# Second expert product of batches 1 to 3 as seven block products with block sums, experts summed in PSUM, gates in the relu outputs

## Chip, cores, metric

The kernel runs on one core of one Trainium2 chip. Times are device microseconds (us) of whole executions, given as the median over the runs of a kernel; executions of one kernel mostly agree within 0.5%. The profile's span, from the first to the last instruction, is about 2 us shorter than the time.

Names: PE is TensorE (PEld its weight loads), DVE is VectorE, ACT is ScalarE, POOL is GpSimd, SP is SyncE. The granted clock is the share of its full speed that PE was allowed. The chain of waits is the work that ended last, followed back at each step to what released it. In all the listings "L592" is a line of the kernel in question, so line numbers differ between kernels.

## The reference, cut to what matters

Sliding-window attention with four sink positions over 4 batches of 768 tokens gives x of 3072 x 512. Then a mixture of four experts, all of them used by every token:

```python
p = domain_probs / (domain_probs.sum(-1, keepdims=True) + 1e-09)   # [3072, 4], never negative
for e in range(4):
    h = np.maximum(x @ w1[e], 0.0)          # 512 -> 1024
    out += p[:, e:e + 1] * (h @ w2[e])      # 1024 -> 512
```

## The kernel before

The kernel interleaves two strands on PE: the attention of the next batch and the two expert products of this batch. A small planner in the Python code keeps a believed clock for each engine and decides, while the program is built, in which order the instructions are recorded. Each engine then executes its own list strictly in that order.

The first product makes h transposed (1024 features on partitions, tokens in the free dimension), the relu writes it to SBUF as `ht`, and the second product uses `ht` as weights, so tokens come out on the partitions, where the gate is one number for a partition:

```python
def emit_first(self):                     # 384 tokens in batches 1 to 3, 256 in batch 0
    for db in range(NDB):
        nc.tensor.matmul(hp_, lhsT=w1_sb[e][:, db, fb*P:(fb+1)*P], rhs=xT[b, db][:, t0:t0+n], ...)
    # relu on whichever of ACT and DVE is believed free first
    ...
def emit_second(self):
    for fb in range(NFB):
        nc.tensor.matmul(op, lhsT=hts[fb][:, off:off+P], rhs=w2_sb[e][:, fb, :], ...)   # 512 columns
    # gate and sum over experts, on DVE, from PSUM:
    nc.vector.scalar_tensor_tensor(out=dst, in0=op, scalar=sc, in1=dst, op0=ALU.mult, op1=ALU.add)
    ...
```

The attention's path from PE to PE crosses DVE twice: the exponentials are multiplied by a mask (`aT`), and the values are divided by their sum (`onat`). PE needs both before it can go on with that strand.

The softmax here doesn't subtract the row's maximum and nothing guards it: scores larger than these inputs give would overflow.

Of the kernel before, what the change touches and what calls it, by code (L numbers as in the profile page):

```python
# [16 lines left out]
def kernel(  # L17
# [42 lines left out]
    PARTS = {b: [(0, G), (G, G), (2 * G, G)] if b == 0 else [(0, 3 * P), (3 * P, 3 * P)] for b in range(B)}  # L60

# [6 lines left out]
    t = {"pe": 0.0, "act": 0.0, "dve": 0.0}  # L68
    bank_free = {tag: [0.0] * n for tag, n in (("mix", 1), ("od", 2), ("h", 2), ("o", 2))}
# [9 lines left out]
    def dve(cols, *deps, rate=0.96):  # L79
        t["dve"] = max(t["dve"], *deps) + 130 + cols / rate  # L80
        return t["dve"] + 60

# [21 lines left out]

    ctx.enter_context(tc.manual_schedule())
# [5 lines left out]
    def load_qk(b, piece):  # L111
        s0, T = PIECES[b][piece]
        for name, src in (("q", q), ("k", k)):
            x = sb.tile([P, H, T * D], BF16, name=f"{name}n", tag=f"{name}n", bufs=1)
            nc.gpsimd.dma_start(
                out=x, in_=src[b, :, s0:s0 + P * T, :].rearrange("h (p t) d -> p h (t d)", t=T),
            )
            nat[b, piece, name] = x
        lands(("qk", b, piece), 2 * H * P * T * D * 4)

    def load_first():

        s0, T = PIECES[0][0]
        for half in range(2):
            hs = slice(4 * half, 4 * half + 4)
            for name, src in (("q", q), ("k", k)):
                x = mo.tile([P, 4, T * D], FP32, name=f"{name}raw", tag=f"osb{half}", bufs=2)
                nc.sync.dma_start(
                    out=x, in_=src[0, hs, s0:s0 + P * T, :].rearrange("h (p t) d -> p h (t d)", t=T),
                )  # L130
                nat[0, half, name, "raw"] = x
            lands(("first", half), 2 * 4 * P * T * D * 4)
# [14 lines left out]
    def regroup(b, piece):  # L147

        s0, T = PIECES[b][piece]
        for name in "qk":  # L150
            x = sb.tile([P, T, H, D], BF16, name=f"{name}o", tag=f"{name}o", bufs=1)
            engine, at = sooner(T * H * D, landed["qk", b, piece], rate=1.9)
            copy(engine, x, nat[b, piece, name].rearrange("p h (t d) -> p t h d", t=T))
            nat[b, piece, name] = x
            grouped[b, piece] = max(at, grouped.get((b, piece), 0))

    def regroup_first():
        s0, T = PIECES[0][0]
        for name in "qk":
            nat[0, 0, name] = sb.tile([P, T, H, D], BF16, name=f"{name}f", tag=f"{name}f", bufs=1)  # L160
        for half in range(2):
            at = max(act(512, landed["first", half]), dve(512, landed["first", half]))
            for name in "qk":
                copy(
                    "act" if name == "k" else "dve",
                    nat[0, 0, name][:, :, 4 * half:4 * half + 4, :],
                    nat[0, half, name, "raw"].rearrange("p h (t d) -> p t h d", t=T),
                )
        grouped[0, 0] = at

    vx = []
    for i in range(2):
        vx.append(consts.tile([P, NQB, H, DP], BF16, name=f"vx{i}"))

    def load_v(b, ts):
        for tb in ts:
            nc.gpsimd.dma_start(  # L177
                out=vx[b % 2][:, tb, :, 0:D],
                in_=v[b, :, tb * P:(tb + 1) * P, :].rearrange("h p d -> p h d"),
            )  # L180
            lands(("v", b, tb), H * P * D * 4)
# [12 lines left out]

    load_first()
    NT = Ntok // P
    dp = consts.tile([NT, P, E], FP32, name="dp")
    nc.sync.dma_start(out=dp, in_=moe_domain_probs.rearrange("(tb p) e -> tb p e", p=P))


    zeros = consts.tile([P, 2 * G], BF16, name="zeros")
# [12 lines left out]
    for i in range(2):  # L214
        nc.vector.memset(vx[i][:, :, :, D:DX], 1.0)
# [44 lines left out]
    vsd = consts.tile([P, B, NHP, 2, DX], BF16, name="vsd")  # L260
# [20 lines left out]
    qkT, xT, sinkA, aTs, onats = {}, {}, {}, {}, {}  # L281
    turned_at, sinkA_at, aT_at, onat_at, xT_at = {}, {}, {}, {}, {}

    def two_banks(tag="mix"):
# [4 lines left out]
        return [psum.tile([P, 2 * G], FP32, name="sps", tag=tag) for _ in range(2)], None  # L289

    def transposes(b, piece, hp, tag="mix"):

        s0, T = PIECES[b][piece]
        if (b, hp) not in qkT:
            qkT[b, hp] = sb.tile([P, 2, S], BF16, name="qkT", tag="qkT", bufs=5)
        tr = psum.tile([P, 2, T, P], BF16, name="tr", tag=tag, bufs=1 if tag == "mix" else 2)
        for i, name in enumerate("qk"):
            for tt in range(T):
                nc.tensor.transpose(tr[:, i, tt], nat[b, piece, name][:, tt, 2 * hp:2 * hp + 2, :], ident)  # L299
        done = pe(2 * T * P, grouped[b, piece], free_at(tag))  # L300
# [8 lines left out]
    def sink_keys(b):  # L309
        for hp in range(NHP):  # L310
            nc.gpsimd.tensor_mul(  # L311
# [3 lines left out]
            )  # L315

    def sink_values(b):
        nc.gpsimd.tensor_mul(
            vsd[:, b], vsf[:, b, None, None, :].to_broadcast([P, NHP, 2, DX]), sel2,
        )  # L320

    def sinks(b, piece):

        if b not in sinkA:
            sinkA[b] = sb.tile([P, 2 * G], BF16, name="sinkA", tag="sinkA", bufs=2)
# [11 lines left out]
        done = pe(q1 - q0 + 300, free_at("mix"), *[turned_at[b, piece, hp] for hp in range(NHP)])  # L337
# [42 lines left out]
    def values(b, hp, g, tag="od"):  # L380

        ready = values_ready(b, hp, g, tag)
        od = psum.tile([P, 2, 2, DX], FP32, name="od", tag=tag)
        a = aTs.pop((b, hp, g))
        cols = 0
        for qi in range(2):
# [7 lines left out]
            if g > 0:  # L394
                nc.tensor.matmul(  # L395
                    od[:, qi], lhsT=sinkA[b][:, (qb - 2) * P:(qb - 1) * P], rhs=vsd[:, b, hp],
# [3 lines left out]
            for ph in range(2):  # L400
                for i, (kb, c) in enumerate(terms):
                    nc.tensor.matmul(  # L402
                        od[:, qi, ph], lhsT=a[:, ph, c:c + P], rhs=vx[b % 2][:, kb, 2 * hp + ph, 0:DX],
# [11 lines left out]
        onats[b, hp, g], onat_at[b, hp, g] = o, at  # L415

    def values_ready(b, hp, g, tag="od"):
        return max(
            aT_at[b, hp, g], free_at(tag), sinkA_at.get((b, g), 0.0), landed["v", b, 2 * g + 1],
        )  # L420

    def turn(b, hp, g, tag="od"):

        o = onats.pop((b, hp, g))
        tx = psum.tile([P, 2, P], BF16, name="tx", tag=tag)
# [10 lines left out]
    def turn_ready(b, hp, g, tag="od"):  # L436
        return max(onat_at[b, hp, g], free_at(tag))

    class Attention:
# [11 lines left out]
        def options(self):  # L451
# [5 lines left out]
            if self.todo:  # L457
# [4 lines left out]
                elif kind == "regroup":  # L462
                    yield max(landed["qk", b, x], t["pe"]), "todo"
                elif kind == "transposes":
                    yield max(grouped[b, x], free_at("mix")), "todo"
                elif kind == "sinks":
                    yield max([free_at("mix")] + [turned_at[b, x, hp] for hp in range(NHP)]), "todo"

        def emit(self, step):
# [7 lines left out]
            else:  # L477
# [4 lines left out]
                elif kind == "regroup":  # L482
                    regroup(b, x)
                    if b > 0:
                        sink_values(b)
                elif kind == "transposes":
                    transposes(b, x, y)
                elif kind == "sinks":
                    if b > 0:
                        sink_keys(b)  # L490
                    sinks(b, x)

# [3 lines left out]
    def gates():  # L496
        pt = psum.tile([P, E, NT], FP32, name="pt", tag="o")
# [9 lines left out]
        take("o", dve(600, pe(400, free_at("o"))))  # L507

    HT = 20
    out_sb = {}  # L510

    class Mixture:


        def __init__(self):
            self.first = [
                (b, e, part, fb) for b in range(B) for e in range(E)
                for part in range(len(PARTS[b])) for fb in range(NFB)
            ]
            self.second, self.hts, self.live, self.since = [], [], 0, 0  # L520
            self.done = 0.0

        def more(self):
            return bool(self.first or self.second)

        def first_ready(self):
            if not self.first or self.live >= HT:
                return 1e12
            b, e, part, fb = self.first[0]
            t0, n = PARTS[b][part]  # L530
            xs = [xT_at.get((b, hp, g), 1e12) for hp in range(NHP) for g in range(t0 // G, (t0 + n - 1) // G + 1)]
            return max(free_at("h"), landed["w1", e], *xs)

        def second_ready(self):
            if not self.second:
                return 1e12
            b, e, tb, hts, off, at = self.second[0]
            return max(free_at("o"), landed["w2", e], at)

        def emit_first(self):  # L540
            b, e, part, fb = self.first[0]
            t0, n = PARTS[b][part]
            ready = self.first_ready()
            self.first.pop(0)
            hp_ = psum.tile([P, n], FP32, name="hps", tag="h")
            for db in range(NDB):
                nc.tensor.matmul(  # L547
                    hp_, lhsT=w1_sb[e][:, db, fb * P:(fb + 1) * P],
                    rhs=xT[b, db][:, t0:t0 + n],
                    start=(db == 0), stop=(db == NDB - 1),  # L550
                )
            end = pe(NDB * n, ready)
            ht = mo.tile([P, n], BF16, name="ht", tag="hT", bufs=HT)
            engine, at = sooner(n, end)
            if engine == "act":
                nc.scalar.activation(out=ht, in_=hp_, func=AF.Relu)  # L556
            else:
                nc.vector.tensor_scalar(out=ht, in0=hp_, scalar1=0.0, scalar2=None, op0=ALU.max)  # L558
            take("h", at)
            self.hts.append((ht, at))  # L560
            self.live += 1
            self.since += 1
            self.done += NDB * n
            if fb == NFB - 1:
                hts = [x[0] for x in self.hts]
                at = max(x[1] for x in self.hts)
                self.hts = []
                for s in range(n // P):
                    self.second.append((b, e, t0 // P + s, hts, s * P, at))

        def emit_second(self):
            ready = self.second_ready()
            b, e, tb, hts, off, _ = self.second.pop(0)
            if (b, 0) not in out_sb:
                for i in range(2):
# [130 lines left out]
```

## Time and profile before

| | before |
|---|---|
| time, median of 3 runs | 420.5 us |
| span of the profiled run | 417.9 us |
| PE / DVE / ACT / POOL busy | 398.6 / 176.0 / 188.7 / 50.1 us |
| mean granted clock of PE | 0.980 |

The page of the kernel before: the span, the first part (busy us of each engine, its share, and the number of instructions) and the engines of the chain of waits.

```profile
span 417.9 us, 7002 instructions
PE 398.6 (95%) x2874; PEld 229.3 (55%) x2918; DVE 176.0 (42%) x349; ACT 188.7 (45%) x336; POOL 50.1 (12%) x94
PE 91%; DMA 3%; ACT 2%; POOL 1%; DVE 1%; issue 1%; ACTq 0%
```

PE is busy 95% of the time and is 91% of the chain, so the kernel is bound by PE and everything else has room. The timeline of PE in a late stretch, where no attention is left (columns: start, duration, engine, line, operation, output and inputs, count):

```profile
331.11 1.89 PE L582 MATMUL mop<-w,ht 128*128 128x512 bf16 x8
332.83 2.91 PE L547 MATMUL hps<-xT,w 128*128 128x384 bf16 x16
335.58 1.89 PE L582 MATMUL mop<-w,ht 128*128 128x512 bf16 x8
```

From the starts, eight 512-column products take 332.83 - 331.11 = 1.72 us, 215 ns each, and sixteen 384-column ones 2.75 us, 172 ns each. Other groups of eight of the latter take 1.30 us, 162 ns each. The groups that the change touches, and two others (columns: busy us, mean ns of one; then idle time before and what ended it):

```profile
L582 PE MATMUL mop<-w,ht 128*128 128x512 bf16 x724 | 174.5, 379 | 3.3 <-issue 1.4
L592 DVE SCALAR_TENSOR_TENSOR out_sb<-mop,scale_t,out_sb 128x512 f32<-128x512 f32 x72 | 54.0, 750 | 106.9 <-PE mop L582 105.8
L363 DVE TENSOR_TENSOR aT<-aT,mask 128x1024 bf16<-128x1024 bf16 (+1 forms) x46 | 31.2, 678 | 50.9 <-ACT aT L362 50.7
L318 POOL TENSOR_TENSOR vsd<-vsf,sel 128x520 bf16<-128x520 f32 x4 | 4.7, 1173 | 0.6 <-DMA vsf<-in_v_dram 0.6
```

The mean of a PE matmul in such a line (379 ns) is longer than the 215 ns between starts, so products overlap in time; what one costs is the distance between starts.

### The profile page before, as it was taken

How to read it: one execution, taken by the hardware profiler on the slowest of the kernel's cores; microseconds unless marked ns; L12 is line 12 of the kernel's file. 1: busy time of each engine (PE TensorE's matmuls, PEld its weight loads, DVE VectorE, ACT ScalarE, POOL GpSimd, SP SyncE). 2: the span in 40 equal slices, each digit the busy share in tenths (PEclk: the TensorE clock that was granted, in tenths of full speed). 3: DMA queues.
4: the chain of work that ended last, by engine and by line, in shares of the span. 5: the costliest groups of instructions: out<-in, count | busy, mean ns of one | idle time of the engine just before them, and what ended most of it. 6: DMA issues, size and time to landing. Idle time of an engine off the chain costs nothing.

```text
span 417.9 us, 7002 instructions
## 1 busy us (share of the span) xinstructions
PE 398.6 (95%) x2874; PEld 229.3 (55%) x2918; DVE 176.0 (42%) x349; ACT 188.7 (45%) x336; POOL 50.1 (12%) x94
## 2 busy tenths in 40 slices
PE   6598899999999999999999999999999999999996
PEld 2366566666676555555555555555555555555552
DVE  3666655565564446343333444334334222222222
ACT  3556315473641554445544645355534333333331
POOL 8745120440000044000000000000000000000000
PEclk9599899999999999999999999999999999999999
DMA  9999999292011129200002100000001100000012
GB/s 175 191 194 209 206 182 164 28 184 17 2 41 61 52 28 184 18 0 2 0 2 77 76 2 0 2 0 2 2 0 56 72 27 0 2 0 2 0 51 100
DMA packets 47428, 25.16 MB, mean 60 GB/s; under 512 B 29965, under 2 KB 42253, under 8 KB 47397
## 3 DMA queue, kind: packets, MB, share of 16 engines
q0 software_dynamic: 41632, 17.30, 33.4%
q1 hardware_dynamic: 5764, 7.42, 5.1%
q8 instruction: 22, 0.36, 0.3%
q14 instruction: 10, 0.07, 0.1%
HBM read 35.73 MB, written 6.29 MB: 101 GB/s over the span
## 4 chain that ended last, share of the span: by engine, by line
PE 91%; DMA 3%; ACT 2%; POOL 1%; DVE 1%; issue 1%; ACTq 0%
PE hps L547 41%; PE mop L582 39%; PE sps L351 3%; DMA kn<-in_k_dram 3%; PE tr L299 3%; PE od L402 2%; PE tx L427 1%; ACT aT L362 1%; PE od L395 1%; POOL vx L177 0%; ACT qkT L135 0%; DVE ht L558 0%; PE sps L330 0%; DVE aT L363 0%; ACT ko L135 0%
## 5 line engine op out<-in xcount | busy, mean ns | idle before, releaser
L547 PE MATMUL hps<-xT,w 128*128 128x384 bf16 (+1 forms) x1152 | 195.6, 310 | 0.5
L582 PE MATMUL mop<-w,ht 128*128 128x512 bf16 x724 | 174.5, 379 | 3.3 <-issue 1.4
L556 ACT ACTIVATE ht<-hps 128x384 bf16<-128x384 f32 (+1 forms) x222 | 103.0, 470 | 149.3 <-PE hps L547 148.3
L547 PEld LDWEIGHTS <-w 128*128 128x128 bf16 x1152 | 108.2, 98 | 62.3 <-issue 8.4
L582 PEld LDWEIGHTS <-ht 128*128 128x128 bf16 x768 | 73.0, 98 | 77.8 <-issue 2.7
L592 DVE SCALAR_TENSOR_TENSOR out_sb<-mop,scale_t,out_sb 128x512 f32<-128x512 f32 x72 | 54.0, 750 | 106.9 <-PE mop L582 105.8
L363 DVE TENSOR_TENSOR aT<-aT,mask 128x1024 bf16<-128x1024 bf16 (+1 forms) x46 | 31.2, 678 | 50.9 <-ACT aT L362 50.7
L362 ACT ACTIVATE aT<-sps 128x1024 bf16<-128x1024 f32 (+1 forms) x46 | 44.0, 957 | 12.6 <-PE sps L351 12.4
L558 DVE TENSOR_SCALAR ht<-hps 128x256 bf16<-128x256 f32 (+1 forms) x66 | 29.8, 451 | 18.9 <-PE hps L547 16.9
L590 DVE TENSOR_SCALAR out_sb<-mop,scale_t 128x512 f32<-128x512 f32 x24 | 18.0, 750 | 34.9 <-PE mop L582 34.8
L135 ACT COPY qkT<-tr 128x1536 bf16<-128x1536 bf16 (+1 forms) x20 | 21.9, 1098 | 16.5 <-PE tr L299 16.5
L135 ACT COPY xT<-tx 128x256 bf16<-128x256 bf16 x32 | 11.9, 374 | 26.6 <-PE tx L427 26.0
L311 POOL TENSOR_TENSOR ksd<-qkT,half 128x8 bf16<-128x8 bf16 x16 | 3.1, 203 | 170.0 <-ACT qkT L135 170.0
L402 PE MATMUL od<-vx,aT 128*128 128x65 bf16 x352 | 20.9, 197 | 2.4 <-DVE aT L363 2.4
L177 POOL DMA_DIRECT2D vx<-in_v_dram x24 | 21.3, 915 | 9.8 <-DMA w<-in_moe_w_dram 9.8
L402 PEld LDWEIGHTS <-aT 128*128 128x128 bf16 x352 | 17.8, 100 | 6.8 <-DVE aT L363 3.2
L412 DVE TENSOR_TENSOR onat<-od,R 128x256 bf16<-128x256 f32 x48 | 20.4, 424 | 1.7
L351 PE MATMUL sps<-qkT 64*128 64x128 bf16 (+1 forms) x256 | 18.4, 246 | 0.5
L427 PE MATMUL tx<-ident,onat 128*128 128x128 bf16 x96 | 13.7, 228 | 3.7 <-DVE onat L412 3.0
L427 PEld LDWEIGHTS <-onat 128*128 128x128 bf16 x96 | 8.3, 99 | 11.5 <-DVE onat L412 4.7
L351 PEld LDWEIGHTS <-qkT 64*128 64x128 bf16 x256 | 8.0, 96 | 10.9 <-issue 9.1
L395 PE MATMUL od<-vsd,sinkA 128*128 128x130 bf16 x64 | 12.9, 220 | 0.0
(60 smaller groups left out, 119.4 us busy)
## 6 DMA issues: line engine op xcount, KB each, us to landing
w<-in_moe_w_dram POOLq DMA_DIRECT2D x8, 1024.0 KB, 15.3
out_dram<-out_sb SPq DMA_DIRECT2D x24, 256.0 KB
vx<-in_v_dram POOLq DMA_DIRECT2D x24, 128.0 KB, 10.9
qn<-in_q_dram POOLq DMA_DIRECT2D x3, 768.0 KB, 7.8
kn<-in_k_dram POOLq DMA_DIRECT2D x3, 768.0 KB, 10.9
qraw<-in_q_dram SPq DMA_DIRECT2D x2, 256.0 KB
kraw<-in_k_dram SPq DMA_DIRECT2D x2, 256.0 KB
qn<-in_q_dram POOLq DMA_DIRECT2D x2, 256.0 KB, 9.9
```

What stands on the lines that cost most here:

```text
L135: (nc.scalar.copy if engine == "act" else nc.vector.tensor_copy)(out=out, in_=in_)
L177: nc.gpsimd.dma_start(out=vx[b % 2][:, tb, :, 0:D], in_=v[b, :, tb * P:(tb + 1) * P, :].rearrange("h p d -> p h d"),)
L351: nc.tensor.matmul(sps[ph][:, c:c + nq * P], lhsT=T[pr, 1, kb * P:(kb + 1) * P], rhs=T[pr, 0, qb * P:(qb + nq) * P], start=True, stop=True,)
L362: nc.scalar.activation(out=a, in_=both[:, :, 0:w], func=AF.Exp, scale=scale)
L363: nc.vector.tensor_mul(a, a, m[:, None, :].to_broadcast([P, 2, w]))
L402: nc.tensor.matmul(od[:, qi, ph], lhsT=a[:, ph, c:c + P], rhs=vx[b % 2][:, kb, 2 * hp + ph, 0:DX], start=(g == 0 and i == 0), stop=(i == l ...
L427: nc.tensor.transpose(tx[:, qi], o[:, qi], ident)
L547: nc.tensor.matmul(hp_, lhsT=w1_sb[e][:, db, fb * P:(fb + 1) * P], rhs=xT[b, db][:, t0:t0 + n], start=(db == 0), stop=(db == NDB - 1),)
L556: nc.scalar.activation(out=ht, in_=hp_, func=AF.Relu)
L558: nc.vector.tensor_scalar(out=ht, in0=hp_, scalar1=0.0, scalar2=None, op0=ALU.max)
L582: nc.tensor.matmul(op, lhsT=hts[fb][:, off:off + P], rhs=w2_sb[e][:, fb, :], start=(fb == 0), stop=(fb == NFB - 1),)
L592: nc.vector.scalar_tensor_tensor(out=dst, in0=op, scalar=sc, in1=dst, op0=ALU.mult, op1=ALU.add,)
```

## The change

The intent is to take work from PE, the engine that bounds the kernel. For batches 1 to 3, two blocks of 128 tokens form a pair. For each pair the product of h (2 token blocks x 2 halves of the features) with w2 (2 halves of the features x 2 halves of the columns) is done in seven block products instead of eight, a Strassen-Winograd scheme, at the price of sums of blocks. To keep the number of sums and of PSUM copies small, all four experts are added up in PSUM. Then the gate can no longer be applied after the second product. It is multiplied into h behind the relu, where tokens lie in the free dimension, so each gate multiply is an elementwise product with a gate row broadcast to all partitions.

```diff
+def weight_forms(e):                       # once for each expert, on GpSimd
+    nc.gpsimd.tensor_sub(x[:, 1], w[:, 1, 1], w[:, 0, 1])
+    nc.gpsimd.tensor_add(x[:, 0], x[:, 1], w[:, 0, 0])
+    nc.gpsimd.tensor_sub(x[:, 2], w[:, 1, 0], x[:, 0])
 ...
 # emit_first: now always 256 tokens, two feature blocks in one PSUM bank
+    if by_act <= by_dve and by_pool <= by_dve + 2500:
+        r = mo.tile([P, 2, G], FP32, name="hr", tag="hr", bufs=2)
+        nc.scalar.activation(out=r, in_=h, func=AF.Relu)
+        nc.gpsimd.tensor_mul(dst, r, gate)                     # dst is a part of H
+    else:
+        nc.vector.scalar_tensor_tensor(out=dst, in0=h, scalar=0.0, in1=gate, op0=ALU.max, op1=ALU.mult)
 ...
+def sums(self):                            # for each expert of a pair, on VectorE
+    nc.vector.tensor_add(S[0][:, e], H21, H22)
+    nc.vector.tensor_sub(H21, H11, H21)
+    nc.vector.tensor_sub(S[1][:, e], S[0][:, e], H11)
+    ...
+    nc.vector.tensor_sub(S[2][:, e], self.H[b, g, e][:, 1, :, 0], S[1][:, e])
 ...
-        nc.tensor.matmul(op, lhsT=hts[fb][:, off:off + P], rhs=w2_sb[e][:, fb, :], ...)
-    nc.vector.scalar_tensor_tensor(out=dst, in0=op, scalar=sc, in1=dst, ...)
+CHAIN = ("P1", "P2", "P6", "P5", "P7", "P4", "P3")
+def emit_product(self):                    # one of the seven, all four experts
+    for i in range(E * QF):
+        e, f = divmod(i, QF)
+        nc.tensor.matmul(x, lhsT=self.operand(b, g, e, m)[:, f], rhs=forms[e][m][:, f], ...)   # 256 columns
+    # P1, P6, P7, P4 are copied out by ACT while one bank goes on accumulating; P2, P5, P3 are added by DVE
```

The rest of the diff (PSUM banks shared between attention and first product, loads of q and k split into head pairs, one buffer of v instead of two, gate rows through a small DRAM tensor) makes room for this.

## The prediction

> **What bounds the kernel now.** TensorE. The page's first part gives PE 398.6 of 417.9 us (95%); the chain of waits is 91% PE, 41% the first expert product and 39% the second. The list of waits shows only about 11 us of PE waiting. VectorE is busy 176, ScalarE 189, GpSimd 50 us: all have room. In the timeline of the last 80 us, eight 512-column products take 1.73 us (216 ns each), eight 384-column ones 1.30 us (162 ns); undisturbed 256-column ones in batch 0 take 109 ns. That is N/2.4 plus about 2.5 ns, as the Trainium skill says (TensorE: Matmul & The Clock Gate, "Wait — 56ns, not 53.3ns?"); this trace agrees. Weight loads, 98 ns each, stay hidden even behind 109 ns.
>
> **What the change does to PE.** Batches 1 to 3, second product: 576 products of 512 columns (124.4 us) become 9 pairs of blocks x 7 x 16 = 1008 of 256 columns (109.9 us): minus 14.5. First product: 768 of 384 columns (124.7 us) become 1152 of 256 (125.6 us): plus 0.9. Net 13.6 us, practically all on the critical path. Batch 0 and attention keep their products. A perfect result would be about 407 us.
>
> **What it adds elsewhere.** VectorE: out goes the gated accumulation of 512 columns (72 x 750 ns = 54 us) and nearly all relu of batches 1 to 3; in come 144 block sums of 512 bf16 elements. The mask multiplies (355 ns at 384 elements, 692 at 1024) put one at about 0.42 us, together 61 us, plus 27 small PSUM adds and 18 gated relus. ScalarE: 126 relus of 512 (about 0.6 us) instead of 222 smaller ones. GpSimd: the built order gives it 126 of the 144 gate multiplies. A similar 520-element multiply took 1.17 us, so an estimate of 146 us, plus 12 weight-block sums (about 27 us). GpSimd rises to about 220 us and becomes a link of the chain relu, gate, sums, block product.
>
> **How much is given back.**
> 1. Bursts. In the last stage the order has 10 to 11 blocks of the first product in a row, one per 0.87 us on PE, while a gate multiply takes about 1.17. Four PSUM banks and two relu buffers absorb some; the first block product then waits for the last gates. The Trainium skill (SBUF — State Buffer, "Practical consequences") says a VectorE instruction with two SBUF inputs contends with a GpSimd one that reads SBUF. The trace before does not show it; sums and gate multiplies are such a pair. I expect 0 to 1 us per pair of blocks, 3 us in all.
> 2. The end: the last seven block products run with no other PE work between. Relu, gate and sums are exposed, and the copy that P4 awaits after P7: about 2.5 us.
> 3. The start of batch 1, which needs all weight sums: 0 to 2 us.
>
> In the middle of these, 407 + 4.5 = 411.5 us; range 406 to 419.
>
> **What the profile would show.** 256-column block products at 109 ns start to start; PE busy down 10 us or more; gate multiplies about 1.2 us and GpSimd busy near 220 us; PE waits on gates or sums of about 1 us at first block products; a tail with short PE gaps. If gate multiplies take 1.5 us or sums 0.8 us, the sharing of the port is real and costs.
>
> **What would make it wrong.** Gate multiplies and sums stretched by each other, so that every pair stalls 2 us or more: 420 and above. In-order VectorE held by a sum waiting for a gate, delaying attention's masks. Or better overlap: 407.
>
> Chances: faster by over 2% (below 412.1) 0.53, within 2% 0.43, slower by over 2% 0.04.

## The result, and the profile after

| | before | after |
|---|---|---|
| time, median of 4 runs each | 420.44 us | 452.19 us |
| ratio | | 1.076 (95% interval 1.0739 to 1.0781) |
| PE / DVE / ACT / POOL busy | 398.6 / 176.0 / 188.7 / 50.1 us | 401.5 / 249.4 / 203.5 / 248.8 us |
| mean granted clock of PE | 0.980 | 0.945 |

The change is slower by 7.6%. A ratio here is the mean time of one kernel's runs over that of the other's of the same rounds, so it is not quite the ratio of the medians. The same lines of the page, now of the changed kernel:

```profile
span 450.8 us, 8881 instructions
PE 401.5 (89%) x3722; PEld 317.8 (70%) x3734; DVE 249.4 (55%) x435; ACT 203.5 (45%) x329; POOL 248.8 (55%) x235
PE 61%; DVE 18%; POOL 10%; DMA 4%; issue 4%; ACT 3%; DVEq 0%; POOLq 0%; ACTq 0%
```

PE fell from 91% of the chain to 61%; DVE and POOL, 2% together before, are now 28%, although each is busy only 55% of the span. An engine with 45% idle time cannot be short of capacity on average, so this is about waits and not about load. The groups of the changed kernel that matter (for the first, the gate multiply, then the four block sums, the mask multiply, and the gated relu that DVE does itself):

```profile
L675 POOL TENSOR_TENSOR H<-hr,gates 128x512 bf16<-128x512 f32 x126 | 166.6, 1339 | 153.2 <-ACT hr L672 99.7
L709 DVE TENSOR_TENSOR S<-H 128x512 bf16<-128x512 bf16 x36 | 27.9, 774 | 68.8 <-POOL H L675 47.5
L710 DVE TENSOR_TENSOR H<-H 128x512 bf16<-128x512 bf16 x36 | 30.0, 832 | 1.2
L711 DVE TENSOR_TENSOR S<-S,H 128x512 bf16<-128x512 bf16 x36 | 26.8, 743 | 0.0
L723 DVE TENSOR_TENSOR S<-H,S 128x512 bf16<-128x512 bf16 x36 | 25.4, 720 | 0.8
L450 DVE TENSOR_TENSOR aT<-aT,mask 128x1024 bf16<-128x1024 bf16 (+1 forms) x46 | 36.4, 794 | 28.7 <-ACT aT L449 28.7
L678 DVE SCALAR_TENSOR_TENSOR H<-hps,gates 128x512 bf16<-128x512 f32 x18 | 12.3, 685 | 5.5 <-PE hps L650 5.3
```

I had put a block sum at 0.42 us. It takes 0.72 to 0.83 us in the mean, together 27.9 + 30.0 + 26.8 + 25.4 = 110.1 us for 144. The mean hides two kinds: in the trace the medians of the last three block sums (L710, L711, L723) are 418 to 426 ns, while their upper quarters begin at 1.37 to 1.48 us. One stretch shows both. First the timeline of DVE in the changed kernel (a bracket is idle time before, and its releaser), then that of POOL, then that of PE:

```profile
196.27 1.48 DVE L709 TENSOR_TENSOR S<-H 128x512 bf16<-128x512 bf16 x1 [3.62 <-POOL H L675]
197.79 1.38 DVE L710 TENSOR_TENSOR H<-H 128x512 bf16<-128x512 bf16 x1
199.09 1.48 DVE L711 TENSOR_TENSOR S<-S,H 128x512 bf16<-128x512 bf16 x1
200.60 1.37 DVE L723 TENSOR_TENSOR S<-H,S 128x512 bf16<-128x512 bf16 x1
201.89 1.61 DVE L450 TENSOR_TENSOR aT<-aT,mask 128x768 bf16<-128x768 bf16 x1
203.43 0.41 DVE L709 TENSOR_TENSOR S<-H 128x512 bf16<-128x512 bf16 x1
```

```profile
192.25 10.84 POOL L675 TENSOR_TENSOR H<-hr,gates 128x512 bf16<-128x512 f32 x8 [1.93 <-ACT hr L672]
```

```profile
197.90 1.05 PE L650 MATMUL hps<-xT,w 128*128 128x256 bf16 x8
203.56 0.51 PE L489 MATMUL od<-vx,aT 128*128 128x65 bf16 x6 [4.62 <-DVE aT L450]
```

From 192.25 to 203.09 us GpSimd runs eight gate multiplies back to back. During that time every block sum of DVE takes as long as one of them; at 203.43, just after GpSimd stops, the same instruction takes 0.41 us. DVE also had to wait 3.62 us for a gate at 196.27 before the first sum. The mask multiply that PE's attention strand needs stands behind the four sums in DVE's list. PE executes its own list in order too, so it stands still for 4.62 us. The list of PE's waits in the whole run, before and then after (columns: who waited for whom, total us, times, longest):

```profile
PE tx L427 <- DVE onat L412: 3.0, 3, 1.9
PE od L402 <- DVE aT L363: 2.4, 3, 1.3
```

```profile
PE tx L515 <- DVE onat L499: 11.7, 10, 4.5
PE od L489 <- DVE aT L450: 10.9, 10, 4.6
PE hps L650 <- DVE H L678: 8.5, 4, 3.2
PE tr L381 <- DVE qkn L154: 5.1, 4, 2.0
```

All the waits in that view add up to 12.4 us before and 43.9 us after. A second loss follows from the first: the mean granted clock fell from 0.980 to 0.945. The Trainium skill (TensorE: Matmul & The Clock Gate, "What's actually happening") says that the clock is at half rate after an idle window of about 3.4 us. Here this trace agrees: its clock records show half rate for 3.4 us from 203.5 us, the end of the 4.62 us wait. But a shorter idle time was enough elsewhere: PE stopped at 239.0 us, for 4.51 us, and the clock records show half rate from 241.0 us, 2.0 us later. Over the run the loss goes from 8.4 us of lost full-speed time (417.9 x 0.020) to 24.8 us (450.8 x 0.055); part of that lies in time in which PE did nothing anyway, so 16 us is an upper estimate for what the clock added. No experiment separates the clock from the waits that cause it.

### The profile page after: what moved, and what is told of

Its sections match the earlier page's. It is cut to its first block, busy times and chain, and to the rows that moved or that the text cites. A ratio compares the mean times of both kernels' runs of the same rounds, so it can differ in the third digit from the quotient of the medians.

```text
span 450.8 us, 8881 instructions
## 1 busy us (share of the span) xinstructions
PE 401.5 (89%) x3722; PEld 317.8 (70%) x3734; DVE 249.4 (55%) x435; ACT 203.5 (45%) x329; POOL 248.8 (55%) x235
## 4 chain that ended last, share of the span: by engine, by line
PE 61%; DVE 18%; POOL 10%; DMA 4%; issue 4%; ACT 3%; DVEq 0%; POOLq 0%; ACTq 0%
PE hps L650 24%; PE acc L757 21%; PE acc L810 8%; POOL H L675 8%; DVE S L709 3%; DVE S L711 3%; DVE H L710 3%; DMA qs<-in_k_dram 3%; DVE aT L450 2%; PE sps L438 2%; PE tr L381 2%; PE od L489 2%; DVE S L723 2%; DVE qkn L154 1%; ACT hr L672 1%
## 5 line engine op out<-in xcount | busy, mean ns | idle before, releaser
L675 POOL TENSOR_TENSOR H<-hr,gates 128x512 bf16<-128x512 f32 x126 | 166.6, 1339 | 153.2 <-ACT hr L672 99.7
L650 PE MATMUL hps<-xT,w 128*128 128x256 bf16 x1536 | 196.4, 282 | 8.7 <-DVE H L678 8.5
L650 PEld LDWEIGHTS <-w 128*128 128x128 bf16 x1536 | 151.1, 101 | 36.0 <-issue 15.1
L672 ACT ACTIVATE hr<-hps 128x512 f32<-128x512 f32 x126 | 75.1, 598 | 102.1 <-PE hps L650 80.9
L709 DVE TENSOR_TENSOR S<-H 128x512 bf16<-128x512 bf16 x36 | 27.9, 774 | 68.8 <-POOL H L675 47.5
L757 PEld LDWEIGHTS <-H 128*128 128x128 bf16 x576 | 55.9, 98 | 8.8 <-DVE H L678 1.1
L810 PE MATMUL acc<-w,H 128*128 128x512 bf16 x180 | 45.0, 389 | 1.0 <-issue 0.5
L757 PEld LDWEIGHTS <-S 128*128 128x128 bf16 x432 | 42.0, 98 | 4.9
L757 PE MATMUL acc<-w,H 128*128 128x256 bf16 x288 | 34.6, 273 | 1.2 <-DVE H L678 0.8
L757 PE MATMUL acc<-wf,H 128*128 128x256 bf16 x288 | 34.4, 273 | 0.5 <-ACT osb L771 0.5
L757 PE MATMUL acc<-w,S 128*128 128x256 bf16 x288 | 34.4, 273 | 0.0
L810 PEld LDWEIGHTS <-H 128*128 128x128 bf16 x192 | 18.5, 100 | 19.2 <-issue 2.1
L489 PE MATMUL od<-vx,aT 128*128 128x65 bf16 x352 | 21.8, 203 | 10.9 <-DVE aT L450 10.9
L710 DVE TENSOR_TENSOR H<-H 128x512 bf16<-128x512 bf16 x36 | 30.0, 832 | 1.2
L711 DVE TENSOR_TENSOR S<-S,H 128x512 bf16<-128x512 bf16 x36 | 26.8, 743 | 0.0
```

Of the source, the lines that this page charges most:

```text
L489: nc.tensor.matmul(od[:, qi, ph], lhsT=a[:, ph, c:c + P], rhs=vx[:, kb, 2 * hp + ph, 0:DX], start=(g == 0 and i == 0), stop=(i == len(term ...
L650: nc.tensor.matmul(h[:, i], lhsT=w1_sb[e][:, db, fb * P:(fb + 1) * P], rhs=xT[b, db][:, g * G:(g + 1) * G], start=(i == 0 and db == 0), st ...
L672: nc.scalar.activation(out=r, in_=h, func=AF.Relu)
L675: nc.gpsimd.tensor_mul(dst, r, gate)
L709: nc.vector.tensor_add(S[0][:, e], H21, H22)
L710: nc.vector.tensor_sub(H21, H11, H21)
```

## The experiments

Three theories. A: GpSimd instructions that read SBUF and DVE instructions with two SBUF inputs shut each other out; DVE, which works in order, holds the attention up. B: the chain from relu over gate and sums to the products is too long for an in-order DVE, whether or not anything contends. C: PE itself is slower with 256-column products. Each run was timed beside the kernel before, whose median was 419.9 to 420.2 us in these rounds.

### e1_write_only: the gate multiply replaced by two writes (wrong result)

```diff
-                    nc.gpsimd.tensor_mul(dst, r, gate)
+                    nc.gpsimd.memset(r, 0.0)
+                    nc.gpsimd.memset(dst, 0.0)
```

> Wrong result on purpose: each of the 126 gate multiplies on GpSimd is replaced by two memsets (one over the relu's buffer, one over H), so GpSimd is busy about as long (about 1.2 us) and every wait and the order of all engines stay, but GpSimd reads nothing from SBUF. Theory A (GpSimd's reads and VectorE's two-input instructions shut each other out): the 144 block sums fall from 0.77 us to 0.42 us, PE's waits for masks and onat mostly go, time 415 to 428 us. Theory B (the chain relu, gate, sums is too long for an in-order VectorE, contention or not): sums may be short, but the time stays near 450 us. Theory C (TensorE itself is slower with 256-column products): stays at 450 us.

Measured: 418.03 us (417.07 to 419.09), relative error 0.80 as intended. That is 34 us less than the changed kernel with the same order on every engine. The groups of GpSimd's replacement, two block sums and the mask in this run (the first sum is the one at L709 above):

```profile
L675 POOL MEMSET hr<- 128x512 f32 x126 | 65.7, 521 | 163.1 <-ACT hr L672 156.8 <-DVE S L724 4.0 <-DVE osb L776 1.6
L676 POOL MEMSET H<- 128x512 bf16 x126 | 65.3, 518 | 0.0
L710 DVE TENSOR_TENSOR S<-H 128x512 bf16<-128x512 bf16 x36 | 15.3, 425 | 71.2 <-POOL H L676 42.1 <-PE acc L758 29.0
L711 DVE TENSOR_TENSOR H<-H 128x512 bf16<-128x512 bf16 x36 | 15.3, 425 | 1.2
L450 DVE TENSOR_TENSOR aT<-aT,mask 128x1024 bf16<-128x1024 bf16 (+1 forms) x46 | 31.7, 688 | 29.4 <-ACT aT L449 29.1
```

GpSimd is still in the chain and still takes 521 + 518 = 1039 ns for each block (against 1339; so 0.3 us of chain is gone too), but the sums are at 0.42 us. Theory A expected 415 to 428 us, B and C about 450. A's mechanism holds, and C is out. DVE still waits 42.1 us for what GpSimd writes before the first sums, against 47.5 in the changed kernel: that wait is nearly all there, and the 34 us are gone without it. PE's waits for masks and values fell from 22.6 to 10.3 us, less than the expected "mostly go". The chain is not quite as long as before, so B gets another test below (e9).

### e2_gates_dve: all gates on DVE

```diff
-                if by_act <= by_dve and by_pool <= by_dve + 2500:
+                if False:
```

> All 144 gate multiplies go to VectorE (one instruction with the relu, 0.69 us), none to GpSimd; the kernel's own planner reorders. Theory A: sums at 0.42 us; VectorE gets about 87 us of gated relus and loses about 50 us of blocking; time 412 to 430 us. Theory B: the chain is shorter by the GpSimd step, so also faster, but VectorE now holds everything in one line: 430 to 445 us. Theory C: 450 us.

Measured: 424.33 us, correct; ratio to the kernel before 1.0091. The sums are at 418 to 425 ns, and DVE is busy 268.6 us, more than the 249.4 us of the changed kernel, yet the run is 28 us faster. So the load on DVE alone was not the trouble. The time lies in A's range and below B's, but this run also takes the GpSimd step out of the chain, so it does not separate blocking from that step.

### e3_no_sums: gates on GpSimd, plain products

```diff
-    CHAIN = ("P1", "P2", "P6", "P5", "P7", "P4", "P3")
+    CHAIN = (0, 1)                       # one product of 32 x 512 columns for each token block
 ... (the weight sums and the block sums are deleted)
+                    x, lhsT=self.H[b, g, e][:, f // QF, f % QF, m], rhs=w2_sb[e][:, f],
```

> The gates stay on GpSimd, but batches 1 to 3 use plain products of 512 columns with four experts summed in PSUM: no weight sums, no block sums. TensorE's own work rises by 14.5 us against the changed kernel. Theory A: with no sums to collide with, gate multiplies fall from 1.34 us to about 1.25 and the attention is held less: 420 to 430 us. Theory B predicts the same, since the sums that wait for gates are gone. Theory C: TensorE has 14.5 us more nominal work and still 1152 first products of 256 columns: above 450 us.

Measured: 429.66 us, correct; ratio 1.0213 (interval 1.0167 to 1.0258). This is inside the 420 to 430 us that A and B both expected, so it does not tell them apart. In this run PE has 14.5 us more nominal work than in the changed kernel, and the run is 22.5 us faster. The planner left 112 of the 144 gate multiplies on GpSimd, at 1.31 us each and not at the expected 1.25. The masks, the largest two-input work that is left on DVE, still suffer: 832 ns at 1024 elements against 692 in the kernel before. So gates on GpSimd cost something even without a single block sum; e8 below, the same plain products with the gates in x, takes 422.15 us, 7.5 less.

### e4_gates_in_x: the gates multiplied into x

Gates are never negative, so relu(gate x w1) equals gate relu(x w1). The gate can be applied to x, which is half as large as h, once for each expert and pair, in bf16 on DVE (the gate rows are stored in bf16 for it); the relus then write H directly, and GpSimd has no gate work.

```diff
+            nc.vector.tensor_mul(x, xTb[b][:, :, g * G:(g + 1) * G], gate)   # 1024 elements, bf16
-                        rhs=xT[b, db][:, g * G:(g + 1) * G],
+                        rhs=xT[b, db][:, g * G:(g + 1) * G] if b == 0 else self.xg[b, g, e][:, db],
-                    nc.gpsimd.tensor_mul(dst, r, gate)
+                nc.scalar.activation(out=dst, in_=h, func=AF.Relu)          # or DVE's max
```

> Since gates are not negative, relu(gate*x*w1) is gate*relu(x*w1): each expert's gate is multiplied into x (36 multiplies of 1024 bf16 elements on VectorE, about 0.69 us each), the relus write H directly, GpSimd has no gate work; block sums stay. Theory A: sums at 0.42 us, no PE wait for VectorE over 2 us in batches 1 to 3, time 407 to 418 us, faster than both. Theory B: also faster than the changed kernel since the chain loses a step, but the 144 sums still stand in VectorE's line: 420 to 440 us. Theory C: 450 us.

Measured: 417.95 us, correct; ratio 0.9931 (0.9894 to 0.9969), at the top of A's range. Sums are at 0.42 us. A's "no PE wait for VectorE over 2 us" was missed: there is one of 2.04 us at 69.01 and one of 2.27 us at 89.46. What was left to find was in one stretch. The engines' busy time from 50 to 100 us in this run, where GpSimd forms the twelve weight sums (columns: PE, PEld, DVE, ACT, POOL busy us with counts, granted clock, DMA share, GB/s):

```profile
50.00:100.00 50.00, 42.45 (x332) 28.07 (x328) 31.93 (x46) 22.66 (x31) 36.48 (x25) 0.90 0.80 107
```

In the trace of this run two DVE copies, each of 768 elements, take 3.70 and 2.27 us at 65.26 and 68.88 us, while GpSimd issues DMAs and then forms the first two weight sums; the same copy took 0.35 us at 62.66.

### e5_gates_in_x_wsums_dve: and the weight sums on DVE

The diff is shortened; the calls are the same with the engine changed.

```diff
-        nc.gpsimd.tensor_sub(x[:, 1], w[:, 1, 1], w[:, 0, 1])      # and two more, for each expert
+        nc.vector.tensor_sub(x[:, 1], w[:, 1, 1], w[:, 0, 1])      # recorded one at a time, when DVE is believed free
```

> The kernel with the gates in x, and its 12 weight sums moved from GpSimd (2.2 us each, 26.7 us, between 66 and 94 us of that run) to VectorE, so GpSimd has no two-input work after the start. That run still lost 14.5 us of PE time between 50 and 100 us, against 5.5 in the kernel before. Theory A (any GpSimd instruction that reads SBUF blocks VectorE's two-input and 2-port work): that stretch falls to 6 to 8 us and the time to 407 to 412 us, 2 to 3% faster than the kernel before. Rival (the stretch is slow because of the late landing of data or the new order of loads): stays at 416 to 419 us.

Measured: 408.41 us (408.18 to 410.11), correct; ratio to the kernel before 0.9724 (0.9700 to 0.9749). It beats both kernels: 2.8% below the kernel before and 44 us below the changed one. The page's first two lines, then the same stretch:

```profile
span 408.4 us, 8656 instructions
PE 386.4 (95%) x3734; PEld 310.2 (76%) x3734; DVE 205.4 (50%) x478; ACT 204.4 (50%) x334; POOL 56.0 (14%) x97
```

```profile
50.00:100.00 50.00, 46.84 (x389) 31.20 (x389) 29.74 (x61) 24.38 (x37) 10.15 (x14) 0.97 0.80 110
```

In the same 50 us PE now gets through 389 products instead of 332, and is idle for 3.2 us instead of 7.6. PE's waits in the whole run add up to 16.8 us, against 12.4 in the kernel before. The largest:

```profile
PE tx L530 <- DVE onat L514: 4.9, 7, 2.4
PE tr L396 <- DVE qkn L154: 3.2, 3, 1.5
PE od L504 <- DVE aT L465: 3.1, 6, 1.0
```

### e6_all_write_only: gates and weight sums as writes (wrong result)

```diff
 (as e1, and)
-        nc.gpsimd.tensor_sub(x[:, 1], w[:, 1, 1], w[:, 0, 1])      # and two more
+        nc.gpsimd.memset(x[:, i], 0.0)                             # twice for each
```

> Wrong result on purpose: the order of the changed kernel untouched, and both the gate multiplies and the 12 weight sums on GpSimd replaced by memsets of about the same length, so that GpSimd reads nothing from SBUF after the start. Against the run with only the gates replaced (418.0 us): theory A says another 6 to 9 us less, 409 to 412 us. The rival (late data, order of loads) says 417 to 419 us.

Measured: 410.12 us (409.02 to 410.94), relative error 0.86 as intended. The order of every engine is that of the changed kernel, and GpSimd is busy 198.8 us of 409.2. Taking away its reads (and with them 0.3 us of each gated block and of each weight sum) recovers 452.19 - 410.12 = 42 us: 34.2 for the gates (e1), 7.9 more for the weight sums. This is also within 2 us of e5, so the late landing of data and the new order of loads are not what slowed that stretch.

### e7_planner_knows: the planner told what a blocked sum costs

```diff
-                    dve(QF * P, self.H_at[b, g, e], rate=1.9, fixed=100)
+                    dve(QF * P, self.H_at[b, g, e], rate=1.9, fixed=1050)
```

> The changed kernel with one number of its planner changed: a block sum is planned at 1.32 us (its length while GpSimd multiplies gates) instead of 0.37. The operations stay the same, only their order and the split of gates between GpSimd and VectorE move. If the loss is only that the plan believed a wrong cost: 420 to 432 us. If the blocking itself takes the capacity (theory A): 440 to 455 us.

Measured: 442.51 us, correct; ratio 1.054. That is in theory A's 440 to 455 us. Block sums take 0.80 to 0.94 us in the mean, and GpSimd has 131 gate multiplies instead of 126. The same operations in an order planned with the right length of a sum are 10 us faster than the changed kernel and still 22 us slower than the kernel before. So a wrong belief in the plan was a part of the loss, and the larger part stays with a plan that knows one right number. This tried one number only; a planner that modelled the exclusion itself might do better, and that stays open.

### e8_gates_in_x_no_sums: gates in x, plain products

The edits of e3 and e4 together.

> Gates in x, no GpSimd two-input work, and plain second products of 512 columns with four experts summed in PSUM: what is left of the change without the seven block products. TensorE's nominal work is 14.5 us above the run with the seven products. Theory A: PE stalls as in the kernel before (34 us in all), so 419 to 424 us; against the seven products without GpSimd work (expected 407 to 412) the block products are worth 9 to 14 us. If the sums' load on VectorE eats their gain, this run is at 410 to 414 us.

Measured: 422.15 us, correct; ratio 1.005. Against e5, which differs by the seven block products and their sums, this is 13.7 us more. So the block products are worth what they take from PE (an estimate of 14.5 us from 216 and 109 ns), as long as GpSimd stays off SBUF reads. Everything else in the change, with gates in x, is worth nothing by itself: 422 against 420 us.

### e9_idle_reads: e5 plus GpSimd reads that nobody needs

```diff
+            for i in (0, 1, 2, 3, 0, 1, 2, 3):
+                nc.gpsimd.tensor_mul(scratch, x[:, i], x[:, i])    # x: the gated x of an expert
```

> The fastest run so far (gates in x, weight sums on VectorE, 408.4 us) plus GpSimd work that nothing uses: for each expert of each pair eight multiplies of 256 elements that read the gated x and write a scratch tile, 288 in all, estimated at 0.6 to 0.7 us each from 2.2 us for 1024. No relu, sum or block product waits for them (only the reuse of the gated x's buffer two experts later does). Theory A (reads on GpSimd block VectorE, no matter who needs their result): block sums from 0.42 to 0.6 to 0.9 us, time 420 to 440 us. Theory B (the loss was the longer chain through GpSimd): 408 to 411 us.

Measured: 429.50 us, correct; 21 us more than e5. The groups of the added multiplies and of two block sums:

```profile
L656 POOL TENSOR_TENSOR scratch<-xg 128x256 bf16<-128x256 bf16 x288 | 196.0, 681 | 108.4 <-DVE xg L652 74.9
L730 DVE TENSOR_TENSOR S<-S,H 128x512 bf16<-128x512 bf16 x36 | 23.3, 646 | 0.0
L742 DVE TENSOR_TENSOR S<-H,S 128x512 bf16<-128x512 bf16 x36 | 20.3, 565 | 1.5 <-DMA out_dram<-osb 0.6
```

No sum waits for these multiplies, and the sums rise from 0.42 to 0.56 to 0.65 us. So blocking needs no dependency, and theory B as the whole explanation falls. The 21 us is not all blocking: one wait of PE of 6.9 us comes from a load of q whose issue stood behind added multiplies in GpSimd's list. About 14 us stay when it is taken out, so it does not bring the run back to B's 408 to 411 us.

## Why the prediction was wrong

1. "What bounds the kernel now": right. PE with 95% busy and 91% of the chain.
2. "Net 13.6 us, practically all on the critical path": right in size. The block products' part of it, 14.5 us, measured 13.7 us (e8 against e5). The 256-column products go at 109 ns from start to start, and their weight loads, 98 ns each, stay hidden.
3. "GpSimd rises to about 220 us": 248.8. The gate multiply took 1.34 us instead of 1.17, the weight sums 2.2 us each as expected.
4. "Put one [block sum] at about 0.42 us, together 61 us": right for a sum left alone (60.3 us in e6: 15.3 + 15.3 + 15.0 + 14.7), wrong for this kernel (110.1 us).
5. **The step that failed** is the first of "How much is given back": "I expect 0 to 1 us per pair of blocks, 3 us in all". The mechanism was named, with the pair of instructions, but priced at 3 us. It measured 42 us (e6 against the changed kernel): 34.2 us from the gates, which is 3.8 us for each of the nine pairs, and 7.9 us from the weight sums. Two things were missed in the pricing. I looked for the stall where gates and products meet, at the first block product, where it is at most 0.8 us. It sat in what else DVE serves: PE waited for values, masks and regrouped q and k of the attention (11.7 + 10.9 + 5.1 us), and for PSUM banks whose gated relu was late on DVE (8.5 us). In all PE's waits are 43.9 us, against 14.1 in e6; the rest of the 42 us lies with the lower clock (0.945 against 0.987), as far as the two can be told apart. And I left the twelve weight sums, 26.5 us of GpSimd reading, out of the contention altogether.
6. "The end: about 2.5 us": about right; the last seven products show gaps of 0.41, 0.83 and 0.46 us, 1.7 in all. "The start of batch 1: 0 to 2 us" was the 50 to 100 us stretch, which lost more: 7.9 us by e6 against e1, for the reason above.
7. "If gate multiplies take 1.5 us or sums 0.8 us, the sharing of the port is real and costs": the second condition came true (0.72 to 0.83). "In-order VectorE held by a sum waiting for a gate, delaying attention's masks" also came true, written down as what would make it wrong and then given a chance of 0.04.
8. "The trace before does not show it": it did. On DVE a mask of 768 elements, 0.56 us elsewhere, took 0.86 us while GpSimd ran its 1.22 us multiply:

```profile
160.47 0.86 DVE L363 TENSOR_TENSOR aT<-aT,mask 128x768 bf16<-128x768 bf16 x1
```

```profile
159.69 1.22 POOL L318 TENSOR_TENSOR vsd<-vsf,sel 128x520 bf16<-128x520 f32 x1
```

The mask began at 160.47, GpSimd ended at 160.91, and the mask ended 0.42 us after that. With only four such multiplies before and 126 of them after, this was the line to look for. Another mask of 768 elements took 1.48 us at 156.61, while GpSimd only issued DMAs; three others beside DMA issues took 0.56 us, and no run here explains this one.

## What to carry to other kernels

Before elementwise work is moved to GpSimd, ask what DVE does at the same time: where both read two operands from SBUF, each held the other up here (a sum took 1.4 us instead of 0.42, a multiply 1.44 instead of 1.26), and whatever stands behind in DVE's list pays. An idle share of 45% on an engine says nothing about how late one urgent instruction in its list comes. Then ask whether the work can move to a smaller operand, so that the contention need not be solved. Here the gates could go past the relu into x, because they are never negative; with that and the weight sums on DVE, the same seven products are 2.8% faster than the kernel before.

## What the Trainium skill lacked or had wrong

- SBUF — State Buffer ("Practical consequences") has the rule, and these runs agree: sums with two SBUF inputs went from 0.42 to about 1.4 us beside GpSimd multiplies, stayed at 0.42 us beside GpSimd memsets (e1, e6), and the gated relu with one input in PSUM stayed at 685 ns with the multiplies (changed kernel) and without (e2).
- The page says that the one that issues second blocks fully. It lacks what two busy engines do to each other: in the stretch shown they alternate, one instruction each. DVE's took 1.37 to 1.48 us instead of 0.42; GpSimd's multiply took 1.44 us in that stretch instead of 1.26. The engine with short instructions lost far more. It is not always one for one: a sum at 155.41 us waited for two multiplies and took 2.69 us.
- Where it speaks of GpSimd issuing DMAs, it warns that DVE starves them. That the issuing holds up a DVE copy is missing: in e4 a copy that takes 0.35 us elsewhere began at 65.26 us, before any weight sum, and took 3.70 us, through DMA issues until 66.58 and then a weight sum until 68.73. In e6 one took 0.81 us beside DMA issues alone (at 66.45).
- GPSIMD Engine Reference ("Elementwise — side-by-side cycle accounting") gives times of two-input work. The warning about DVE stands elsewhere on that page ("Key points") and has no size. In e9, 288 multiplies whose results nobody used cost 21 us, about 14 without the late load of q.
- VectorE: DVE Perf Modes ("The perf-mode tier table") gives lengths of a tensor_tensor alone; the page has no note that they hold only without GpSimd reads (0.42 against a mean of 0.72 to 0.83 us here).
